# Linear attention and a squared-ReLU FFN on one core: a reordered start, empty matmuls in TensorE's waits, six output buffers and a last sum in three column runs

## The chip, the cores and the metric

The kernel runs on one core of a Trainium2 chip. A core has TensorE (matrix multiply, PE in the profile; its weight loads are PEld), VectorE (DVE), ScalarE (ACT), GpSimd (POOL) and SyncE (SP, which only issues DMAs here). TensorE writes to PSUM, which here is eight banks of 128 x 512 fp32; VectorE and ScalarE read it. The metric is the device time of the core in microseconds (us), given as the median of runs without a profile.

## The reference

Four batches of eight heads, 768 steps, head size 48. Each head keeps a 48 x 48 state:

```python
for t in range(S):
    cur = einsum('bhd,bhe->bhde', u * kt, vt)
    y[:, :, t] = einsum('bhd,bhde->bhe', rt, state + cur)
    state = w * state + einsum('bhd,bhe->bhde', kt, vt)
x = y.transpose(0, 2, 1, 3).reshape(3072, 384)
h = maximum(x @ w_in, 0)          # w_in 384 x 2048
out = h * h @ w_out               # w_out 2048 x 384
```

## The kernel before

The 768 steps are cut into six chunks of 128, so with four batches there are 24 *units*, numbered chunk by chunk: units 0 to 3 are the first chunk of each batch. A unit's 128 rows of x are 128 tokens of the FFN.

The whole program is one written list, `ORDER`. Each word is a step of one engine, `name.unit:engine/buffers`: `Y.0:P/5` is step Y of unit 0 on TensorE (P) into bank 5; D is VectorE, A ScalarE, G GpSimd, S SyncE. A loop at the end of the kernel calls the function of that name in class `Do`. So the list gives the order in each engine's queue, and each engine works its queue strictly in that order; semaphores hold a step until its inputs are there and its buffer is free. Nothing is rearranged by a scheduler.

The attention part of one unit:

- `ld.r`, `ld.k`, `ld.v` (L388) load 192 KB each. `rh`, `kh` (L434, L428) scale r and k by powers of w; `P0`, `P1`, `du` (L437, L441, L444) form sum(r * u * k) per head and `dv` (L449) multiplies it with v; `vb` (L286 on ScalarE, L288 on VectorE and GpSimd) is v in bf16.
- `T` (L464) transposes scaled r and k on TensorE into PSUM and `Tc` copies them out; later units use a transposing DMA, `XB`, instead.
- `A` (L494) makes the 128 x 128 products of each head, the heads of even number in one bank and those of odd number in another; `Bm` (L507, VectorE, one for each of the two banks) masks them. "Block A of unit 2" is `A.2`.
- `Y` (L531) multiplies the masked blocks with v, and from unit 4 on adds the state's part (L527); `xs` (L560, VectorE) adds dv and gives x; `U` (L552) makes the unit's update of the state.
- `X` (L578) transposes x on TensorE and `xTc` copies it out; later units use a DMA, `xX` (L585).

The FFN goes by groups: unit 0, unit 1, then two units at a time. `F1.g.s` (L594) makes four 128-wide blocks of the hidden layer (two where the group has two units), `re` (L602, L604) applies ReLU, `sq` (L609, L613) squares, `F2` (L622) sums over the hidden layer in PSUM, `os` copies the sum to a buffer in SBUF (pool `os`), and `out` (L667) stores it. The last unit to be summed, 22, is done by `F2c` (L636), column run by column run, so that the first run is copied and stored while the next is summed.

The weights arrive in the start: `lW.0.s` (L396) loads a 384 KB piece of w_in into one of six staging buffers and `cW.0.s` casts it to bf16 into W1_s. A staging buffer is loaded again only when its cast is done: `lW.0.3` uses the buffer of `lW.0.5` and so follows `cW.0.5`. W1_2 and w_out are loaded by GpSimd's DMAs (L418 to L422).

`Z.n.b` (L648, L650) is empty work: matmuls of the identity into bank b, n / 4 of them 512 columns wide and the remainder 128 wide. The kernel before has Z.66.7 and Z.22.7 ahead of T.3 and A.0.

Of the kernel before, what the change touches and what calls it, by code (L numbers as in the profile page):

```python
# [22 lines left out]
POOLS = dict(ldr=7, ldk=7, ldv=7, st=6, rk=7, P0=5, dv=5, vb=8, rkT=7, Bm=6, xs=5, hr=6, hq=30, os=4, ts=2, xT1=2, xT2=3)  # L23
# [57 lines left out]
P0.17:G/0 P1.17:G ts.16:D/0 du.17:D/2 sq.8.6:A0/28 F2.12.0.4:P/6 os.12:D/3 S.16:G Bm.17.0:D/1 U.13:P/3 ts.13:D/0 ld.v.19:S/5  # L81
# [3 lines left out]
re.8.4:A/3 F2.14.4.4:P/7 F2.15.12.4:P/1 F2.14.0.4:P/7 S.15:D ld.v.20:S/3 sq.8.4:A0/8 F2.15.8.4:P/1 os.15:A/2 U.14:P/2  # L85
ts.14:D/0 F2.14.8.4:P/7 os.14:A/0 kh.22:G/2 Bm.19.1:D/4 xX.17:S/1 F1.9.2:P/3 P1.21:G re.9.2:A/2 F1.9.6:P/5 re.9.6:A/4
# [7 lines left out]
F1.10.1:P/7 re.10.3:A/2 XB.22:S/6 os.16:D/2 Bm.20.1:D/4 sq.10.3:D2/11 re.10.1:A/5 F2.17.12.4:P/2 ld.v.22:S/0 os.17:D/1  # L94
# [4 lines left out]
S.18:G Y.22:P/7 F2.18.12.4:P/0 os.18:A/3 F1.11.4:P/2 re.11.4:A/5 P0.22:D/1 P1.22:D du.22:D/2 du.23:D/4 F1.11.6:P/5  # L99
# [3 lines left out]
F1.12.0:P/5 sq.11.0:D2/26 F2.20.0.4:P/1 F1.12.2:P/2 re.12.2:D/5 F1.11.3:P/7 re.11.2:A/1 sq.11.2:A0/3 os.19:D/0 F2.21.0.4:P/4  # L103
# [3 lines left out]
os.20:A/2 out.20:S F2.23.0.4:P/7 F2.23.8.4:P/7 os.23:D/0 os.21:A/3 out.21:S F2c.22.0:P/2 os.22.0:D/1 F2c.22.1:P/6 os.22.1:D/1  # L107
out.23:S out.22.0:A out.22.1:S
# [12 lines left out]
def kernel(  # L121
# [13 lines left out]
    B, H, S, D = r.shape  # L135
# [5 lines left out]
    d_model, d_ff = moe_w_in.shape  # L141
# [171 lines left out]
    class Do:  # L313
# [315 lines left out]
        def F2c(e, i, h):  # L629
            g, j = group_of[i]  # L630
            n = len(GROUP[g])
            m = 4 // n
            c = part(h)
            for f in range(FCH):
                at = L * n * (f % m) + L * j
                e.matmul(  # L636
                    bank(f"bO{i}{h}")[:, c],
                    hqb[slot[f"hq{g},{f // m}"]][:, at : at + L],
                    W2[f // 4][:, f % 4, c],
                    start=(f == 0), stop=(f == FCH - 1), skip_group_check=True,  # L640
                )
# [10 lines left out]
        def os(e, i, half=None):  # L652
            c = part(half)
            o = f"bO{i}" if half is None else f"bO{i}{half}"
            copy(e, osb[slot[f"os{i}"]][:, c], bank(o)[:, c])

        def out(e, i, half=None):
            c = part(half)
            t = osb[slot[f"os{i}"]]
            if i < PAIRED:  # L660
                o = bass.AP(
                    tensor=out.tensor, offset=out.offset + ((i - i % 2 + half) * S + i % 2) * d_model,
                    ap=[[2 * d_model, L // 2], [1, d_model]],
                )
                e.dma_start(out=o, in_=t[rows[half], :])
            else:
                e.dma_start(out=out_v[(i % B) * NCH + i // B][:, c], in_=t[:, c])  # L667
# [56 lines left out]
```

## Time and profile before

| | |
|---|---|
| median of three runs | 173.69 us (172.4 to 175.07) |
| profiled execution | 171.62 us |
| its span, first to last instruction | 169.9 us |
| mean granted TensorE clock | 0.99 |
| TensorE busy | 160.1 us, 94% |
| VectorE busy | 140.3 us, 83% |
| ScalarE busy | 104.4 us, 61% |
| GpSimd busy | 87.4 us, 51% |
| moved by DMA | 29.13 MB, mean 171 GB/s |

Start times in the profile are microseconds from the first instruction. A timeline row has start, duration, engine, line, operation, output <- input, and the number of instructions merged into it; behind it stands, in brackets, the idle time of the engine ahead of it and who ended that. "Granted clock" is TensorE's clock as a share of full speed. Durations of matmuls include the drain of the last one, so rows of TensorE overlap a little.

### The profile page before, as it was taken

The page shows a single profiled execution, that of the slowest core. Times are in us where ns is not written, and L with a number is a line of the kernel's source. Part 1 is how long each engine was busy: PE and PEld are TensorE (multiplying, and loading weights), DVE is VectorE, ACT ScalarE, POOL GpSimd, SP SyncE. Part 2 cuts the span into 40 slices and gives each one's busy share as a digit, 9 for nine tenths or more (in the row PEclk, how much of TensorE's full clock was granted, in tenths as well). Part 3 has the DMA queues.
Part 4 walks back from the last instruction along what each step waited for, and adds up shares of the span by engine and source line. Part 5 has one row for each costly group of instructions (what it writes and reads, how often), then busy time and mean ns, then how long its engine had stood idle before and what let it go on. Part 6 is the DMA issues. An engine that isn't in the chain of part 4 may idle for free.

```text
span 169.9 us, 4338 instructions
## 1 busy us (share of the span) xinstructions
PE 160.1 (94%) x1691; PEld 121.2 (71%) x1691; DVE 140.3 (83%) x272; ACT 104.4 (61%) x187; POOL 87.4 (51%) x105
## 2 busy tenths in 40 slices
PE   3974999999999999999999989999999999999993
PEld 1443888867787777787786776977786785878872
DVE  5599978869999997798999899899879889682731
ACT  3566497791799483766398273695595544644640
POOL 5427966308584699994649104869722862000000
PEclk9999699999999999999999999999999999999999
DMA  5999999997698999999979897999973954120422
GB/s 102 226 257 309 315 206 205 218 209 146 117 220 135 223 205 247 228 173 205 228 151 215 198 175 153 218 160 221 133 160 80 138 116 132 25 80 0 143 93 93
DMA packets 105588, 29.13 MB, mean 171 GB/s; under 512 B 98008, under 2 KB 105568, under 8 KB 105568
## 3 DMA queue, kind: packets, MB, share of 16 engines
q1 hardware_dynamic: 103272, 26.56, 77.0%
q0 software_dynamic: 1744, 1.77, 6.5%
q10 hardware_dynamic: 552, 0.53, 1.1%
q8 instruction: 13, 0.21, 0.5%
q14 instruction: 7, 0.06, 0.1%
HBM read 20.46 MB, written 4.72 MB: 148 GB/s over the span
## 4 chain that ended last, share of the span: by engine, by line
PE 78%; DMA 9%; DVE 4%; ACT 3%; issue 2%; POOL 1%; SPq 1%; POOLq 0%
PE bank L622 32%; PE bank L594 32%; PE bank L494 3%; DMA st<-in_moe_w_in_dram 3%; DMA ldv<-in_v_dram 2%; PE bank L531 2%; DMA ldk<-in_k_dram 2%; DMA rkT<-rk 2%; PE bank L578 2%; PE bank L527 2%; PE bank L552 2%; PE bank L636 2%; PE bank L464 1%; DVE Bm L507 1%; ACT rkT L286 1%
## 5 line engine op out<-in xcount | busy, mean ns | idle before, releaser
L594 PE MATMUL bank<-xT,W 128*128 128x256 bf16 (+1 forms) x624 | 71.1, 265 | 0.0
L622 PE MATMUL bank<-W,hq 128*128 128x384 bf16 x368 | 68.7, 326 | 0.1
L594 PEld LDWEIGHTS <-W 128*128 128x128 bf16 x624 | 56.2, 98 | 8.4 <-DVE W L288 0.2
L602 ACT ACTIVATE hr<-bank 128x512 bf16<-128x512 f32 x70 | 40.6, 593 | 25.8 <-PE bank L594 25.2
L609 ACT ACTIVATE hq<-hr 128x512 bf16<-128x512 bf16 x72 | 43.6, 627 | 7.8 <-DVE hr L604 6.6
L622 PEld LDWEIGHTS <-hq 128*128 128x128 bf16 x368 | 34.1, 98 | 18.6 <-ACT hq L609 0.7
L507 DVE TENSOR_TENSOR Bm<-bank,maskJT 128x512 bf16<-128x512 f32 x48 | 31.1, 679 | 0.9 <-PE bank L494 0.9
L604 DVE TENSOR_SCALAR hr<-bank 128x512 bf16<-128x512 f32 x26 | 17.6, 686 | 10.3 <-PE bank L594 9.5
L441 POOL TENSOR_TENSOR P<-P,ub 128x384 f32<-128x384 f32 x14 | 14.7, 1051 | 17.4 <-DVE P L437 17.0
L434 POOL TENSOR_TENSOR rk<-ldr,Wt 128x384 bf16<-128x384 f32 x13 | 14.2, 1094 | 5.3 <-DMA ldr<-in_r_dram 5.3
L449 POOL TENSOR_TENSOR dv<-ldv,du 128x384 f32<-128x384 f32 x16 | 13.6, 856 | 4.0 <-DVE du L444 3.7
L560 DVE TENSOR_TENSOR xs<-bank,dv 128x384 bf16<-128x384 f32 x24 | 13.1, 551 | 2.2 <-PE bank L531 0.7
L286 ACT COPY os<-bank 128x384 f32<-128x384 f32 x13 | 5.9, 483 | 13.5 <-PE bank L622 13.5
L573 POOL TENSOR_TENSOR S0W<-ts,WLm 128x384 bf16<-128x384 f32 x9 | 9.4, 1051 | 8.6 <-DVE ts L570 8.5
L428 POOL TENSOR_TENSOR rk<-ldk,Wkhat 128x384 bf16<-128x384 f32 x12 | 13.0, 1089 | 0.4 <-DMA ldk<-in_k_dram 0.3
L444 DVE TENSOR_REDUCE du<-P 128x8 f32<-128x384 f32 x24 | 12.9, 544 | 0.2
L613 DVE TENSOR_TENSOR hq<-hr 128x512 bf16<-128x512 bf16 x24 | 12.5, 525 | 0.4
L531 PE MATMUL bank<-vb,Bm 128*128 128x48 bf16 x192 | 11.5, 186 | 1.1 <-ACT vb L286 1.1
L288 POOL CAST vb<-ldv 128x384 bf16<-128x384 f32 x10 | 5.7, 568 | 13.1 <-DMA ldv<-in_v_dram 13.1
L437 POOL TENSOR_TENSOR P<-ldr,ldk 128x384 f32<-128x384 f32 x10 | 10.3, 1031 | 3.1 <-DMA ldr<-in_r_dram 3.1
L531 PEld LDWEIGHTS <-Bm 128*128 128x128 bf16 x192 | 9.8, 98 | 2.1 <-DVE Bm L507 1.2
L494 PE MATMUL bank<-rkT 48*128 48x128 bf16 x192 | 8.0, 221 | 2.4 <-ACT rkT L286 1.8
(67 smaller groups left out, 161.0 us busy)
## 6 DMA issues: line engine op xcount, KB each, us to landing
ldr<-in_r_dram SPq DMA_DIRECT2D x24, 192.0 KB, 3.7
ldk<-in_k_dram SPq DMA_DIRECT2D x24, 192.0 KB, 3.6
ldv<-in_v_dram SPq DMA_DIRECT2D x24, 192.0 KB, 4.2
out_dram<-os SPq DMA_DIRECT2D x23, 192.0 KB, 2.3
st<-in_moe_w_in_dram SPq DMA_DIRECT2D x6, 384.0 KB, 5.4
W<-in_moe_w_out_dram POOLq DMA_DIRECT2D x4, 384.0 KB, 6.5
st<-in_moe_w_in_dram ACTq DMA_DIRECT2D x1, 384.0 KB
rkT<-rk SPq DMA_TRANSPOSE x17, 3.7
```

The lines of the kernel that those rows point to most:

```text
L434: e.tensor_mul(scaled("r", i), loaded("r", i), early("WtQ") if i < EARLY else Wt2)
L441: e.tensor_mul(t, t, ub)
L449: e.tensor_mul(dvb[slot[f"dv{i}"]], loaded("v", i), t)
L494: e.matmul(heads(bank(f"bA{i}{h}"), 128)[:, hc, :], t[p0 : p0 + D, HP + hc, :], t[p0 : p0 + D, hc, :], start=True, stop=True, skip_group_c ...
L507: e.tensor_mul(o, a, mask_b)
L531: e.matmul(y[:, hc, D * h : D * (h + 1)], m[h][:, hc, :], vb[:, 2 * hc + h, :], start=(i < B), stop=True, skip_group_check=True,)
L560: e.tensor_add(xsb[slot[f"xs{i}"]].rearrange("p (a b) -> p a b", a=HP), heads(bank(f"bY{i}"), 2 * D), dvb[slot[f"dv{i}"]].rearrange("p (a ...
L594: e.matmul(hp[:, fi, :], W1[f // 2][:, c, 128 * (f % 2) : 128 * (f % 2 + 1)], xt[:, c, :], start=(c == 0), stop=(c == CCH - 1), skip_group ...
L602: e.activation(hr, hp, AF.Relu)
L604: e.tensor_scalar_max(hr, hp, 0.0)
L609: e.activation(hq, hr, AF.Square)
L622: e.matmul(bank(f"bO{i}")[:, 0:d_model], hqb[slot[f"hq{g},{f // m}"]][:, at : at + L], W2[f // 4][:, f % 4, :], start=(summed[i] == 1), st ...
```

## The change

Four things change.

1. The order of the first units. On VectorE, `Bm.0.0` comes ahead of `Bm.1.0`, and `xs.0` (the sum of unit 0) ahead of both Bm of unit 3. On TensorE, `A.2` comes ahead of `U.0`, and `X.0` (the transpose that gives x of unit 0) ahead of `Y.3`; X.0 and Y.1 use other banks. On ScalarE, `vb.0` and `Tc.2` come ahead of `cW.0.5`.
2. Five new empty steps: Z.20.7 ahead of A.1, Z.10.6 ahead of A.3, Z.8.0 ahead of U.3, Z.8.5 ahead of Y.0, Z.8.2 ahead of Y.3; in all 13 matmuls of 512 columns and 2 of 128.
3. The pool `os` has six buffers for four, and the steps take them in turn.
4. F2c of unit 22 is done in three column runs of 192, 128 and 64 for two of 256 and 128. The second run is copied and stored by ScalarE, the first and third by VectorE and SyncE.

```diff
-POOLS = dict(ldr=7, ldk=7, ldv=7, st=6, rk=7, P0=5, dv=5, vb=8, rkT=7, Bm=6, xs=5, hr=6, hq=30, os=4, ts=2, xT1=2, xT2=3)
+POOLS = dict(ldr=7, ldk=7, ldv=7, st=6, rk=7, P0=5, dv=5, vb=8, rkT=7, Bm=6, xs=5, hr=6, hq=30, os=6, ts=2, xT1=2, xT2=3)
...
-A.0:P/4/5 ld.k.2:S/3 WtS:A lW.0.5:A/1 P1.3:G kh.1:D/2 lW.0.1:S/0 rh.1:D/2 T.1:P/6 Tc.1:A/1 A.1:P/7/3 Tc.3:A/2 A.3:P/6/2 ld.v.0:S/0
+A.0:P/4/5 ld.k.2:S/3 WtS:A lW.0.5:A/1 P1.3:G kh.1:D/2 lW.0.1:S/0 rh.1:D/2 T.1:P/6 Tc.1:A/1 Z.20.7:P A.1:P/7/3 Tc.3:A/2 Z.10.6:P A.3:P/6/2 ld.v.0:S/0
...
-        return slice(0, d_model) if half is None else (slice(0, 256), slice(256, d_model))[half]
+        return slice(0, d_model) if half is None else (slice(0, 192), slice(192, 320), slice(320, d_model))[half]
```

The first place is VectorE's queue where the Bm steps of units 0, 1 and 3 stand. Bm_0 and Bm_2 are the two blocks of unit 0 (Bm.0.1 and Bm.0.0), Bm_1 and Bm_5 those of unit 1, Bm_3 and Bm_4 those of unit 3; xs_0 and xs_1 are the sums of units 0 and 3, and xT1_0 is x of unit 0, transposed. Before:

```order
L507 TENSOR_TENSOR Bm_0_121<-bank_5_190,maskJT_239 128x512
L507 TENSOR_TENSOR Bm_1_122<-bank_7_192,maskJT_239 128x512
L507 TENSOR_TENSOR Bm_2_123<-bank_4_189,maskJT_239 128x512
L507 TENSOR_TENSOR Bm_3_124<-bank_2_187,maskJT_239 128x512
L507 TENSOR_TENSOR Bm_4_125<-bank_6_191,maskJT_239 128x512
L560 TENSOR_TENSOR xs_0_127<-bank_5_190,dv_0_101 128x384
L507 TENSOR_TENSOR Bm_5_126<-bank_3_188,maskJT_239 128x512
L560 TENSOR_TENSOR xs_1_128<-bank_2_187,dv_1_102 128x384
L288 COPY xT1_0_132<-bank_6_191 128x384
```

After (the last number of a name only counts buffers, and is two higher behind the new ones):

```order
L507 TENSOR_TENSOR Bm_0_121<-bank_5_192,maskJT_241 128x512
L507 TENSOR_TENSOR Bm_2_123<-bank_4_191,maskJT_241 128x512
L507 TENSOR_TENSOR Bm_1_122<-bank_7_194,maskJT_241 128x512
L560 TENSOR_TENSOR xs_0_127<-bank_5_192,dv_0_101 128x384
L507 TENSOR_TENSOR Bm_3_124<-bank_2_189,maskJT_241 128x512
L507 TENSOR_TENSOR Bm_4_125<-bank_6_193,maskJT_241 128x512
L507 TENSOR_TENSOR Bm_5_126<-bank_3_190,maskJT_241 128x512
L560 TENSOR_TENSOR xs_1_128<-bank_2_189,dv_1_102 128x384
L288 COPY xT1_0_132<-bank_5_192 128x384
```

The sum of unit 0 moved from the sixth place to the fourth; the copy of its transposed x stays ninth.

The second place is ScalarE's queue at the same time: rkT_1, rkT_2 and rkT_3 are the copies Tc of units 1, 3 and 2, vb_1 is vb.0, W1_5 and W1_0 are cW.0.5 and cW.0.0. Before:

```order
L286 COPY rkT_1_115<-bank_6_191 128x1024
L286 COPY rkT_2_116<-bank_2_187 128x1024
L286 CAST W1_5_198<-st_1_180 128x768
L286 CAST vb_1_107<-ldv_0_77 128x384
L286 COPY rkT_3_117<-bank_1_186 128x1024
L286 CAST W1_0_193<-st_2_181 128x768
```

After:

```order
L286 COPY rkT_1_115<-bank_6_193 128x1024
L286 COPY rkT_2_116<-bank_2_189 128x1024
L286 CAST vb_1_107<-ldv_0_77 128x384
L286 COPY rkT_3_117<-bank_1_188 128x1024
L286 CAST W1_5_200<-st_1_182 128x768
L286 CAST W1_0_195<-st_2_183 128x768
```

The cast of the weight piece W1_5 moved behind the two copies that had stood behind it.

The third place is the end of SyncE's queue, the last stores (os_1 is the buffer of unit 22 in both). Before:

```order
L667 DMA out_0_dram<-os_1_174 128x384
L667 DMA out_0_dram<-os_2_175 128x384
L667 DMA out_0_dram<-os_3_176 128x384
L667 DMA out_0_dram<-os_0_173 128x384
L667 DMA out_0_dram<-os_1_174 128x128
```

After:

```order
L667 DMA out_0_dram<-os_5_178 128x384
L667 DMA out_0_dram<-os_2_175 128x384
L667 DMA out_0_dram<-os_3_176 128x384
L667 DMA out_0_dram<-os_1_174 128x192
L667 DMA out_0_dram<-os_1_174 128x64
```

The first run of unit 22 is now stored by SyncE, which ended with a run of 128 columns and now ends with one of 64; the run that ScalarE stores is 128 columns wide and was 256.

More of the change, by code (lines that the diff above doesn't have):

```diff
@@ L106 @@
 re.12.1:D/5 F1.12.5:P/5 sq.12.1:D2/0 F2.20.4.4:P/1 re.12.6:A/4 sq.12.6:A0/4 F2.23.12.4:P/7 re.12.5:A/2 sq.12.5:A0/12 out.17:S
-os.20:A/2 out.20:S F2.23.0.4:P/7 F2.23.8.4:P/7 os.23:D/0 os.21:A/3 out.21:S F2c.22.0:P/2 os.22.0:D/1 F2c.22.1:P/6 os.22.1:D/1
-out.23:S out.22.0:A out.22.1:S
+os.20:A/5 out.20:S F2.23.0.4:P/7 F2.23.8.4:P/7 os.23:D/3 os.21:A/2 out.21:S F2c.22.0:P/2 os.22.0:D/1 F2c.22.1:P/6 os.22.1:A/1 F2c.22.2:P/0 os.22.2:D/1
+out.23:S out.22.0:S out.22.1:A out.22.2:S
 """
```

30 lines of the change are left out of this document (15 added, 15 removed).

## The prediction

> **What bounds the kernel now.** I read the page's busy line and its slices first, then the list of who waited for whom on TensorE, then a table of time windows over the start, and last the timelines of the engines there. Four rows of the page:
>
> ```profile
> PE 160.1 (94%) x1691; PEld 121.2 (71%) x1691; DVE 140.3 (83%) x272; ACT 104.4 (61%) x187; POOL 87.4 (51%) x105
> ...
> PE   3974999999999999999999989999999999999993
> ...
> DVE  5599978869999997798999899899879889682731
> ...
> PEclk9999699999999999999999999999999999999999
> ```
>
> The second row is TensorE in 40 slices of 4.25 us: after the fifth slice it is full until the last one. All its waits on other engines are these (total us, times, longest):
>
> ```profile
> PE bank L494 <- ACT rkT L286: 1.8, 3, 1.1
> PE bank L531 <- ACT vb L286: 1.1, 1, 1.1
> PE bank L494 <- DMA rkT<-rk: 0.5, 1, 0.5
> PE bank L552 <- POOL vb L288: 0.5, 1, 0.5
> ```
>
> Only the 0.5 us for a DMA lies behind the start. So the kernel is a TensorE stream with a start in front and a tail behind: a microsecond won before the stream is full moves the end, and so does one won in the tail; nothing between has room. The windows over the start (columns: PE, PEld, DVE, ACT, POOL busy with instruction counts, granted clock, DMA share, GB/s):
>
> ```profile
> 9.50:12.90 3.40, 2.28 (x31) 1.29 (x28) 3.37 (x9) 2.85 (x4) 1.00 (x1) 1.00 1.13 270
> 12.90:16.35 3.45, 1.33 (x27) 1.17 (x28) 3.45 (x7) 1.94 (x4) 2.63 (x5) 1.00 1.14 309
> 16.35:19.75 3.40, 3.19 (x48) 2.60 (x45) 3.40 (x8) 1.88 (x3) 3.32 (x4) 0.51 1.14 314
> 19.75:23.20 3.45, 3.43 (x66) 3.25 (x63) 3.45 (x7) 2.70 (x7) 2.54 (x4) 0.99 1.21 257
> ```
>
> Two readings. TensorE is busy only 1.33 of 3.45 us in the second window, and in the third it is granted half its clock. And VectorE is busy through all of the last three. The second reading decides what the first is worth. VectorE's timeline (start, us, line, out<-in):
>
> ```profile
> 13.31 0.94 DVE L288 CAST W<-st 128x768 bf16<-128x768 f32 x1
> 14.17 3.07 DVE L507 TENSOR_TENSOR Bm<-bank,maskJT 128x512 bf16<-128x512 f32 x5
> 17.16 0.55 DVE L560 TENSOR_TENSOR xs<-bank,dv 128x384 bf16<-128x384 f32 x1
> 17.63 0.68 DVE L507 TENSOR_TENSOR Bm<-bank,maskJT 128x512 bf16<-128x512 f32 x1
> 18.23 0.54 DVE L560 TENSOR_TENSOR xs<-bank,dv 128x384 bf16<-128x384 f32 x1
> 18.69 0.34 DVE L288 COPY xT<-bank 128x384 bf16<-128x384 bf16 x1
> ...
> 21.36 1.80 DVE L288 CAST W<-st 128x768 bf16<-128x768 f32 x2
> 23.08 0.55 DVE L560 TENSOR_TENSOR xs<-bank,dv 128x384 bf16<-128x384 f32 x1
> 24.06 0.36 DVE L288 COPY xT<-bank 128x384 bf16<-128x384 bf16 x1 [0.44 <-PE bank L578]
> ```
>
> Each row starts before the one ahead has ended; the first idle time is the 0.44 us at 24.06. And TensorE:
>
> ```profile
> 9.15 1.24 PE L648 MATMUL bank<-identity 128*128 128x512 bf16 x5
> 14.44 0.61 PE L464 MATMUL bank<-identity,rk 128*128 128x128 bf16 x8
> 16.20 0.38 PE L531 MATMUL bank<-vb,Bm 128*128 128x48 bf16 x8 [1.15 <-ACT vb L286]
> 19.12 1.17 PE L594 MATMUL bank<-xT,W 128*128 128x128 bf16 x12
> 23.69 0.34 PE L578 MATMUL bank<-identity,xs 128*128 128x128 bf16 x3
> 23.86 4.78 PE L594 MATMUL bank<-xT,W 128*128 128x128 bf16 x54
> ```
>
> The first F1 (19.12) starts when VectorE's copy of xT (18.69 + 0.34) is done, and the transposes X.2 (23.69) when VectorE's xs.2 (23.08 + 0.55 = 23.63) is done. From 23.86 TensorE has its work lined up. **The start ends at 23.86, and VectorE, not TensorE and not its clock, sets that moment.**
>
> **Part 1, the order of unit 0.** On VectorE the change permutes the stretch from 14.17 to 19.03: six Bm, two xs and one xT copy, the same nine before and after, and everything behind stays. A queue that never waits ends at the same time in any order, so the gain at 23.86 is 0, unless a moved step now waits. The two that could: xs.0 is now fourth. The five Bm take (3.07 - 0.68) / 4 = 0.60 us each, so the second (Bm.0.0) ends at 14.17 + 0.60 + 0.68 = 15.45 and the third at 16.05. Y.0 needs Bm.0.0 and vb.0; it takes 0.38 us from about 15.5, so its sum is there at 15.9, before the third Bm ends. xs.3 stays where it was (18.23), but its Y.3 starts only when Bm.3.0 ends, now sixth: 17.16 + 0.55 = 17.71. With 0.38 us for Y.3 that is 18.1 at full clock: 0.1 us to spare. Price 0; bounds 0 to +0.4 (both waits, at half clock).
>
> **Part 2, the empty matmuls.** Five wide ones took 1.24 us with the last one's drain, about 0.21 each, narrow ones a quarter of that. Added are 1.07 us ahead of A.1 (wait 1.1), 0.54 ahead of A.3 and 0.43 ahead of U.3 (waits of about 0.5 each), and 0.43 ahead of Y.0, behind T.2 (about 14.9) and Bm.0.1 (14.85), so done by 15.3 to 15.4, before 15.5. The last 0.43 stand ahead of Y.3, behind the read of Bm.3.1 (about 17.1): done by 17.6, before 17.71. Behind each in TensorE's queue stands the very step that waits anyway. Price 0. What they buy is busy time in the window 12.90 to 16.35: 1.33 + 0.43 + 0.43 for those of U.3 and Y.0, part of A.3's, and Y.0 and A.2 moved into it, some 2.7 of 3.45, above the 2.28 after which the clock stayed. So I expect a clock of 1.0 from 16.35 to 19.75. F1.0.0 then takes about 0.7 instead of 1.17 us, and TensorE waits that much longer for VectorE at 23.2: again 0. On when the clock falls, the Trainium skill (TensorE: Matmul & The Clock Gate, section Why this matters for your kernels) asks for no idle gap above about 3 us. Here the longest is 1.15 us and the clock fell all the same, so busy share, not the gap, is what I go by; by the rule the empty matmuls would change nothing, and the sum would be the same.
>
> **Part 3, ScalarE and the queue of SyncE.** vb.0 moves from behind cW.0.5 to ahead of it, and cW.0.5 behind Tc.2:
>
> ```profile
> 11.42 1.93 ACT L286 COPY rkT<-bank 128x1024 bf16<-128x1024 bf16 x2 [0.55 <-PE bank L464]
> 14.85 0.88 ACT L286 CAST W<-st 128x768 bf16<-128x768 f32 x1 [1.51 <-DMA st<-in_moe_w_in_dram]
> 15.64 0.51 ACT L286 CAST vb<-ldv 128x384 bf16<-128x384 f32 x1
> 16.05 1.01 ACT L286 COPY rkT<-bank 128x1024 bf16<-128x1024 bf16 x1
> ```
>
> vb.0 can run from 13.35; Tc.2 when T.2 is done (14.44 + 0.61 = 15.05), to about 16.1; cW.0.5 then ends at 16.95 instead of 15.73. cW.0.0 behind it starts at 16.95 in both. But cW.0.5 frees the staging buffer into which SyncE loads lW.0.3, and all of SyncE's later loads queue behind that one:
>
> ```profile
> 16.18 1.30 SPq L396 DMA_DIRECT2D st<-in_moe_w_in_dram  x1
> ```
>
> It could not start before about 16.95: 0.75 us of hold. Its data is first needed by cW.0.3 on GpSimd, and that by F1.2.3:
>
> ```profile
> 23.36 0.82 POOL L288 CAST W<-st 128x768 bf16<-128x768 f32 x1 [1.05 <-DMA st<-in_moe_w_in_dram]
> ```
>
> In the run of 54 F1 matmuls from 23.86, F1.2.3 comes behind 12 narrow and 6 wide ones, a share of 1.3 us by columns (24 narrow and 30 wide fill 4.6), so at 25.2. cW.0.3 ended at 24.18 and would end at 24.93: 0.25 us to spare. Price 0, bounds 0 to +1.05 (the 1.30 of that issue added to the hold, less the 1.0 of slack).
>
> **Part 4, six output buffers.** The list of waits names no copy to os that waited for a store: the ones on record wait for TensorE. Only addresses and slots change; I take 0, and a gain or loss is bounded by the absence of such a wait, so 0 both ways.
>
> **Part 5, the tail.** F2c.22 runs in 256 and 128 columns now, and in 192, 128 and 64 after:
>
> ```profile
> 164.39 2.65 PE bank L636 x32
> ```
>
> That is the chain's row; the copies, the last issue and the landings (kind, count, size, us from the issue) are:
>
> ```profile
> 166.18 0.42 DVE L288 COPY os<-bank 128x256 f32<-128x256 f32 x1 [1.19 <-PE bank L636]
> 167.07 0.29 DVE L288 COPY os<-bank 128x128 f32<-128x128 f32 x1 [0.47 <-PE bank L636]
> ...
> 167.39 0.33 SPq L667 DMA_DIRECT2D out_dram<-os  x1
> ...
> out_dram<-os ACTq DMA_DIRECT2D x1, 128.0 KB, 1.7
> out_dram<-os SPq DMA_DIRECT2D x1, 64.0 KB, 1.5
> ```
>
> The columns are the same 384 per row of weights, 16 times; 2.65 us over 16 x 384 columns is 0.43 ns a column. 16 more matmuls cost at least nothing and, at the 8 matmuls of 48 columns in 0.38 us shown at 16.20 (48 ns each, drain included), at most 16 x (48 - 28) = 0.3 us; I take 0.05, near the first, since loads overlap. The last copy shrinks from 128 to 64 columns: 0.13 us between 256 and 128, so about 0.065 less: 0.22. SyncE's issue and landing then follow as before (0.33, and 1.5 or a little less for half the bytes). The middle piece goes out on ScalarE's queue: matmuls done at 164.39 + 1.33 + 0.88 = 166.6, copy about 0.3, issue about 0.4, landing 1.7: 169.0, before the last piece's 169.2. Price 0.05 - 0.065 = -0.01; bounds -0.2 to +0.3.
>
> **The sum.** 0 + 0 + 0 + 0 - 0.01: the profiled execution stays at a span of 169.9 and 171.62 us. It was the fastest of the four on record (172.40, 173.69, 175.07 beside it; their mean is 173.2, the median given is 173.69), so with no effect I would expect a new median near 173.2; I take 0.2 off for executions in which the clock falls at a worse place (rival C). **Forecast: 173.0 us.**
>
> **Rivals.**
> A. *TensorE paces the start after all.* If VectorE's rows could close up (as they cannot by the row of 3.45 busy of 3.45), the half clock's 3.19 us of work would cost 1.6 less: 171.4. For it speaks the 0.51 clock; against it the 24.06 row. Chance 0.17.
> B. *The hold on SyncE bites: slower.* lW.0.3 lands later than cW.0.3's slack allows, TensorE stops ahead of F1.2.3, and the loads of units 4 and 5 are late behind it. It decides from a hold of 1.0 us; price up to 1.05: 174.0. For it: cW.0.3 already waits 1.05 us for that load. Against: DMA shares above 1 mean a backlog, in which a late issue loses less than it is late. Chance 0.13.
> C. *The place of the clock's fall differs from one execution to the next, and the empty matmuls remove the bad ones.* The second spell of full clock began at this weight load, and 16.35 lies three spells of 3.42 us behind it:
>
> ```profile
> 6.09 1.43 PEld L648 LDWEIGHTS <-identity 128*128 128x128 bf16 x7 [0.28 <-issue]
> ```
>
> Were the half clock two microseconds later, to 21.75, TensorE would lose another 1.0, less some 0.2 of waiting at 23.2: 0.8. Without it 172.2. The Trainium skill (TensorE: Matmul & The Clock Gate, Part 1: The HAM clock gate) has a window of 3413 ns that runs freely and does not start with the kernel; the spacing here agrees, its shift between executions no run here shows. Chance 0.10.
> D. *The change doesn't do what it says*: the clock falls all the same, the empty matmuls take twice as long, Y.3 and xs.3 come 0.4 late: 173.4. Chance 0.05.
>
> The forecast has 0.55. The range is 171.0 to 175.0: it takes in A to D, the bounds of parts 1, 3 and 5, and the runs' own spread of 2.7 us, of which a median of three keeps the larger part. Two per cent is 3.5 us, about what a measurement of this kernel can tell from no change; no case reaches it, so within 2% has 0.92, and the runs' spread leaves 0.04 on each side (below 170.2, above 177.2).
>
> **What the profile after would show.** Right: granted clock 1.0 in the fifth slice; TensorE's L648 rows ending before A.1, A.3, U.3, Y.0, Y.3 start; VectorE without idle time from 8.5 to 23.6, xs.2 ending near 23.6 and the long F1 run starting near 23.9; SyncE's load of lW.0.3 starting near 17.0; the last output copy 0.22 us. Wrong: an xs.2 that ends before 23.2 (A), a wait of PEld for GpSimd's W near 25 (B), an idle VectorE ahead of xs.0 or xs.3 (D), or a later part of the stream that moves although nothing in it was touched.

## The result, and the profile after

The changed kernel takes 174.03 us in the median of 20 runs (172.82 to 176.61), the kernel before 173.19 us in 20 runs beside it (171.76 to 176.73). The ratio is 1.0055, with a 95% interval of 1.0032 to 1.0078: slower by half a per cent, some 0.9 us. I had forecast no change (173.0 us). The profiled execution took 173.70 us, with a span of 172.0 us. Executions more than 1.5% above the fastest of their kernel are left out of every ratio below, and profiles taken in one are left out of the table and the readings.

The page of the changed kernel, busy time and slices as before:

```profile
PE 162.8 (95%) x1722; PEld 121.5 (71%) x1722; DVE 139.4 (81%) x272; ACT 104.6 (61%) x188; POOL 88.4 (51%) x105
...
PE   3996899999999999999999799999999999999993
...
PEclk9999999999999999999999999999999999999999
```

The empty matmuls hold the clock, as forecast: TensorE is fuller in the third and fourth slices, and its granted clock never falls. The windows over the start (columns as before):

```profile
12.90:16.35 3.45, 2.58 (x30) 1.51 (x31) 3.45 (x7) 1.13 (x3) 1.65 (x3) 1.00 1.02 292
16.35:19.75 3.40, 2.56 (x43) 1.52 (x42) 3.08 (x7) 2.33 (x3) 3.32 (x5) 1.00 1.09 308
```

Granted clock 1.00 where it had been 0.51, and 2.58 us of work where there had been 1.33. But VectorE, busy 3.40 of 3.40 us in the second of these windows before, is now busy 3.08. Its timeline says why:

```profile
14.61 1.88 DVE L507 TENSOR_TENSOR Bm<-bank,maskJT 128x512 bf16<-128x512 f32 x3
16.81 0.56 DVE L560 TENSOR_TENSOR xs<-bank,dv 128x384 bf16<-128x384 f32 x1 [0.33 <-POOL dv L449]
17.29 1.88 DVE L507 TENSOR_TENSOR Bm<-bank,maskJT 128x512 bf16<-128x512 f32 x3
...
23.91 0.55 DVE L560 TENSOR_TENSOR xs<-bank,dv 128x384 bf16<-128x384 f32 x1
```

The row at 16.81 is xs.0 in its new place. It waits 0.33 us, and the input that came last was dv.0 on GpSimd, done at 16.78. xs.2 then starts at 23.91 (23.08 before), and the long F1 run at 24.70 (23.86 before):

```profile
24.52 0.34 PE L578 MATMUL bank<-identity,xs 128*128 128x128 bf16 x3
24.70 4.78 PE L594 MATMUL bank<-xT,W 128*128 128x128 bf16 x54
```

The long run is 0.84 us later. Of that, 0.44 was there already when the first Bm started (14.61 for 14.17; nothing ahead of it on VectorE was changed, and the executions differ there), the other 0.40 comes between. The chain that ended last, over this stretch, names the same steps (start, us, what):

```profile
8.77 5.88 DMA ldv<-in_v_dram
14.65 0.05 issue
14.70 0.50 POOL vb L288
15.21 1.58 POOL dv L449 x2
16.79 0.02 issue
16.81 0.56 DVE xs L560
17.37 1.79 DVE Bm L507 x3
19.17 0.46 DVE xs L560
```

The load of v of unit 3, vb.3, dv.3 and dv.0 on GpSimd, then xs.0: in its new slot the sum of unit 0 hangs on the landing of the data of unit 3, because GpSimd works vb.3 and dv.3 ahead of dv.0. TensorE's Y.0, the other input of xs.0, was hardly earlier:

```profile
15.43 0.61 PE L464 MATMUL bank<-identity,rk 128*128 128x128 bf16 x8
15.87 0.59 PE L648 MATMUL bank<-identity 128*128 128x512 bf16 x2
16.31 0.36 PE L531 MATMUL bank<-vb,Bm 128*128 128x48 bf16 x8
```

The last row is Y.0, done at 16.67. Its Bm.0.0 had been done at 15.89 (14.61 + 0.60 + 0.68). But U.3, ahead of T.2 (15.43), had waited 0.9 us for vb.3, and then the two empty matmuls Z.8.5 stood ahead of Y.0: they cost it some 0.4 us, from 15.89 to 16.31. In kernels below where xs.0 does wait for Y.0, it starts 0.10 to 0.11 us behind Y.0's end; here that would be 16.77 or 16.78. So dv.0 and Y.0 were late by nearly the same amount, and both stand behind vb.3.

In the kernel before the chain of the same stretch does not touch VectorE's xs.0:

```profile
16.14 0.92 ACT rkT L286
17.07 0.05 issue
17.11 0.61 PE bank L494 x6
17.72 0.43 PE bank L531 x8
18.15 0.32 PE bank L578 x3
18.47 0.35 PE bank L531 x8
```

Behind 24.70 the changed kernel loses more. Of TensorE's waits (total us, times, longest)

```profile
PE bank L594 <- DMA xT<-xs: 1.6, 3, 1.0
PE bank L552 <- POOL vb L288: 0.9, 1, 0.9
```

the second is that of U.3 in the start, but all three parts of the first lie behind 24.70, the longest at 97.66 us; it is new. From the start of the long F1 run to that of F2c the profile before has 140.37 us and this one 141.77, 1.40 more. In the tail little moves: F2c started at 164.23 before and 166.47 after (+2.24), the last copy ended at 167.36 and 169.58 (+2.22), and from the start of F2c to the end of the span it is 5.67 us before and 5.53 after.

```profile
166.47 2.84 PE L636 MATMUL bank<-W,hq 128*128 128x192 bf16 x48
...
169.35 0.23 DVE L288 COPY os<-bank 128x64 f32<-128x64 f32 x1 [1.00 <-PE bank L636]
```

### The profile page after: what moved, and what is told of

Read it like the earlier page. It is cut to its first block, busy times and chain, and to the rows that moved or that the text cites. A ratio compares the mean times of both kernels' runs of the same rounds, so it can differ in the third digit from the quotient of the medians.

```text
span 172.0 us, 4403 instructions
## 1 busy us (share of the span) xinstructions
PE 162.8 (95%) x1722; PEld 121.5 (71%) x1722; DVE 139.4 (81%) x272; ACT 104.6 (61%) x188; POOL 88.4 (51%) x105
## 4 chain that ended last, share of the span: by engine, by line
PE 56%; DVE 11%; issue 11%; DMA 9%; POOL 6%; SPq 3%; ACT 1%; DVEq 0%; POOLq 0%
PE bank L594 25%; PE bank L622 22%; DVE Bm L507 4%; DMA xT<-xs 4%; DMA ldv<-in_v_dram 3%; SPq L388 3%; DMA ldr<-in_r_dram 2%; PE bank L494 2%; DVE xs L560 2%; PE bank L636 2%; PE bank L531 1%; POOL P L437 1%; POOL rk L434 1%; PE bank L527 1%; DVE W L288 1%
## 5 line engine op out<-in xcount | busy, mean ns | idle before, releaser
L286 ACT COPY os<-bank 128x384 f32<-128x384 f32 (+1 forms) x14 | 6.2, 468 | 16.6 <-PE bank L622 13.8
L437 POOL TENSOR_TENSOR P<-ldr,ldk 128x384 f32<-128x384 f32 x10 | 10.9, 1097 | 3.8 <-DMA ldr<-in_r_dram 3.8
L648 PE MATMUL bank<-identity 128*128 128x512 bf16 x34 | 10.1, 434 | 2.8 <-POOL identity masks.py:199 2.7
L613 DVE TENSOR_TENSOR hq<-hr 128x512 bf16<-128x512 bf16 x24 | 12.0, 506 | 0.3
L531 PE MATMUL bank<-vb,Bm 128*128 128x48 bf16 x192 | 11.0, 183 | 0.2 <-DVE Bm L507 0.2
```

Source lines behind the costliest of these rows:

```text
L531: e.matmul(y[:, hc, D * h : D * (h + 1)], m[h][:, hc, :], vb[:, 2 * hc + h, :], start=(i < B), stop=True, skip_group_check=True,)
```

## The experiments

Each kernel was timed in 12 runs, beside 23 to 35 runs of the kernel before on the same chip; the interval of a ratio is some 0.4% to either side, nearly as much as the effect, so I lean on groups of kernels and on what each profile shows at one place.

### First group: which of the four edits

Theory O: the new order of the first units costs. Theory Z: the empty matmuls cost. Theory S: the six buffers or the column runs cost. Theory H: within O, the later cast cW.0.5 holds SyncE's load lW.0.3 and what queues behind it. (Where these expectations speak of P, it is the chain over GpSimd from vb.3 to the weight loads it issues.)

**e1_order**, the new order alone:

```diff
-ld.v.3:S/1 ... cW.0.5:A T.2:P/1 cW.0.1:D
-Bm.0.1:D/0 Bm.1.0:D/1 vb.0:A/1 Tc.2:A/3 Bm.0.0:D/2 Y.0:P/5 U.0:P/7 Bm.3.1:D/3 A.2:P/1/4 Bm.3.0:D/4 ld.v.1:S/2 Y.3:P/2 dv.0:G
-xs.0:D/0 lW.0.0:S/2 X.0:P/6 ...
+ld.v.3:S/1 ... vb.0:A/1 T.2:P/1 cW.0.1:D Tc.2:A/3 cW.0.5:A
+Bm.0.1:D/0 Bm.0.0:D/2 Y.0:P/5 Bm.1.0:D/1 A.2:P/1/4 U.0:P/7 dv.0:G xs.0:D/0 X.0:P/5 Bm.3.1:D/3 Bm.3.0:D/4 ld.v.1:S/2
+Y.3:P/2 lW.0.0:S/2 ...
```

> The new order of the start alone: no empty matmuls, four output buffers, the last sum in two runs as before. Theory W (xs.0, moved ahead, waits on VectorE for GpSimd's dv.0; 0.33 us in the trace after): slower by 0.2 to 0.6%, and an idle VectorE ahead of xs.0. Theory H (cW.0.5 behind Tc.2 holds SyncE's load of lW.0.3, the loads behind it leave 1 to 2 us later, and transposing DMAs of the middle are late): slower by 0.4 to 0.8%, with SyncE's wc at about 18.4 instead of 17.6 and over 1 us of TensorE waits for DMA. Theory Z (the empty matmuls cost) and theory S (buffers and tail cost): within 0.2% of before.

Measured: 174.55 us for 173.64; ratio 0.9992 (0.9951 to 1.0032). Not resolved by itself: the median of all twelve executions is 0.9 us up, the ratio, to which six of them count, is not.

**e2_empty**, the five empty steps alone:

```diff
+Z.20.7:P   ahead of A.1
+Z.10.6:P   ahead of A.3
+Z.8.0:P    ahead of U.3
+Z.8.5:P    ahead of Y.0
+Z.8.2:P    ahead of Y.3
```

> Only the five empty steps, at the same five places of the old order. Theory Z: slower by 0.4% or more, with steps of the start that begin later behind L648. Theories W, H, S: within 0.2% of before, with a granted clock of 1.0 from 16.35 to 19.75 and the long F1 run at 23.9 all the same, since VectorE sets it; if TensorE's half clock did cost something, faster by up to 0.5%.

Measured: 173.6 for 173.64 us; ratio 0.9983 (0.9949 to 1.0017). No cost or gain that can be measured: Z is not borne out.

**e3_os_tail**, the six buffers and the three column runs alone:

```diff
-... os=4 ...
+... os=6 ...
-F2c.22.1:P/6 os.22.1:D/1 out.23:S out.22.0:A out.22.1:S
+F2c.22.1:P/6 os.22.1:A/1 F2c.22.2:P/0 os.22.2:D/1 out.23:S out.22.0:S out.22.1:A out.22.2:S
```

> Only the six output buffers and the three column runs of the last sum; the start as before. Theory S: slower by 0.4% or more, from stores or from the tail. Theories W, H, Z: within 0.2% of before, the tail (start of F2c to the end of the span) within 0.2 us of before's 5.5 us.

Measured: 172.92 for 173.64 us; ratio 0.9976 (0.9942 to 1.001). S falls. No other kernel came out lower, but the kernel before, measured once more as c1 below, is at 0.9978.

**e4_cast_first**, the whole change with cW.0.5 ahead of Tc.2:

```diff
-vb.0:A/1 T.2:P/1 cW.0.1:D Tc.2:A/3 cW.0.5:A
+vb.0:A/1 T.2:P/1 cW.0.1:D cW.0.5:A Tc.2:A/3
```

> The whole change, but with ScalarE's cast cW.0.5 ahead of Tc.2 (vb.0 stays ahead of both), so that SyncE's load of lW.0.3 is not held. Theory H: the loss goes (within 0.2% of before), wc at about 17.6. Theory W: the loss stays, 0.3 to 0.8% slower than before, with VectorE idle ahead of xs.0. Theories Z and S: the loss stays too.

Measured: ratio 1.0057 (1.0022 to 1.0091). The loss stays, so H is not borne out.

### Second group: the edits in pairs

**e7_empty_os_tail** is the change without the new order, **e8_order_os_tail** without the empty matmuls, **e9_order_empty** without buffers and column runs, **e10_again** the changed kernel unaltered. The edits are those above, combined.

> The change without its new order: the empty matmuls, the six buffers and the three column runs over the old order of the start. Theory O (the new order of the start is what costs, whatever in it): 0.1 to 0.5% faster than before. Theory X (only order and empty matmuls together cost, each alone is harmless): within 0.3% of before. Theory Z (the empty matmuls cost): 0.3% or more slower.

> The change without its empty matmuls: new order, six buffers, three column runs. Theory O: slower than before by 0.2 to 0.6%. Theory X: within 0.3% of before. Theory Z: within 0.3% of before or faster. The granted clock falls to a half for one or two spells of 3.4 us as in before.

> The new order and the empty matmuls, with four buffers and two column runs. Theories O and X: as slow as the whole change or a little slower, 0.4 to 0.8%. Theory S (buffers or tail cost): within 0.3% of before.

> The whole change once more, beside the three others on the same chip, and with a second trace of it: 0.3 to 0.8% slower than before by every theory. In its trace theory W wants VectorE idle ahead of xs.0 for GpSimd's dv.0 again; theory P (GpSimd's whole queue is late behind the load of v for unit 3, and with it the load of the first piece of w_out) wants the first F2 row to start at the moment that load lands, not when the 54 F1 matmuls end.

Measured: e7 1.0022 (0.9987 to 1.0057), e8 1.0063 (1.002 to 1.0107), e9 1.0038 (0.9991 to 1.0084), e10 1.0043 (0.9999 to 1.0086). The three with the new order are up, two of them with an interval that reaches 1; the one without it is not resolved from no change. X falls by e8. O fits best, but it is not shown here: it had e7 faster than the kernel before, and the interval of e7 overlaps those of the other three.

### Third group: which part of the order

Theory V: xs.0, now early on VectorE, waits for dv.0. Theory A: ScalarE's order. Theory P from here on: what is left, Bm.0.0 ahead of Bm.1.0 and A.2 ahead of U.0.

**e5_dv0**, the whole change with dv.0 first on GpSimd:

```diff
-ld.v.3:S/1 vb.3:G/0 ...
+ld.v.3:S/1 dv.0:G vb.3:G/0 ...
-... U.0:P/7 dv.0:G xs.0:D/0
+... U.0:P/7 xs.0:D/0
```

> The whole change, with dv.0 put ahead of vb.3 on GpSimd, so that it is done before the data of v of unit 3 has to be there. Theory V (the new order costs because xs.0, now early on VectorE, waits for dv.0 on GpSimd): no idle time of VectorE ahead of xs.0, the long F1 run starts some 0.3 us earlier against the first Bm (9.7 for 10.1 us), and the time is 0.0 to +0.4 us from the kernel before. Theory A (the order of ScalarE costs) and theory P (the order of TensorE and of the Bm): no idle time ahead of xs.0 either, but the time stays at +0.7 us.

Measured: ratio 1.0053 (1.0013 to 1.0093). And xs.0 still waits, longer than in the changed kernel, and for another engine:

```profile
17.23 0.56 DVE L560 TENSOR_TENSOR xs<-bank,dv 128x384 bf16<-128x384 f32 x1 [0.81 <-PE bank L531]
```

TensorE explains it. U.3 stands ahead of T.2 and Y.0 in its queue and needs vb.3, which GpSimd now does behind dv.0:

```profile
15.71 0.33 PE L552 MATMUL bank<-vb,rk 128*128 128x96 bf16 x4 [0.94 <-POOL vb L288]
...
16.76 0.36 PE L531 MATMUL bank<-vb,Bm 128*128 128x48 bf16 x8
```

Behind U.3 come T.2 and Z.8.5, two empty matmuls that stand ahead of Y.0 from 16.33 to 16.76 here, though Bm.0.0 was done at 15.83. So dv.0 was only one of two inputs of xs.0 that are just in time; with it out of the way, Y.0 is the late one, by its place behind vb.3 and, for 0.43 us of the 0.81, by the empty step. My claim that e5 would have no idle time ahead of xs.0 was wrong.

**e11_xs_late**, the whole change with xs.0 and X.0 back in their old places:

```diff
-... dv.0:G xs.0:D/0 X.0:P/5 Bm.3.1:D/3 Z.8.2:P Bm.3.0:D/4 ld.v.1:S/2
-Y.3:P/2 ...
+... dv.0:G Bm.3.1:D/3 Z.8.2:P Bm.3.0:D/4 xs.0:D/0 ld.v.1:S/2
+Y.3:P/2 X.0:P/5 ...
```

> The whole change, with xs.0 back behind both Bm of unit 3 on VectorE, and X.0 behind Y.3 on TensorE; the order of ScalarE and the rest stay new. Theory V: xs.0 stands where dv.0 has long been done, so the time is 0.0 to +0.3 us from the kernel before. Theories A and P: +0.7 us.

Measured: 175.4 for 174.54 us; ratio 1.0031 (0.9994 to 1.0069). xs.0 has no wait, but the time does not decide: the interval holds both no change and the whole loss.

**e12_act_old**, the whole change with cW.0.5 ahead of vb.0 and Tc.2 as before:

```diff
-du.1:D/2 vb.0:A/1 T.2:P/1 cW.0.1:D Tc.2:A/3 cW.0.5:A
+du.1:D/2 cW.0.5:A vb.0:A/1 T.2:P/1 cW.0.1:D Tc.2:A/3
```

> The whole change, with ScalarE's order as before (cW.0.5 ahead of vb.0 and Tc.2). Theory A: 0.0 to +0.2 us from the kernel before. Theories V and P: +0.7 us. vb.0 is then done at about 16.1, so Y.0 and xs.0 come later than in the kernel changed, and by V the stall ahead of xs.0 is as long or longer, only with TensorE as the one waited for.

Measured: ratio 1.0076 (1.0042 to 1.011); xs.0 waits 0.58 us for Y.0, as V has it. A alone falls.

**e13_dv0_later**, the whole change with dv.0 behind vb.1 on GpSimd:

```diff
-U.0:P/7 dv.0:G xs.0:D/0 ... vb.1:G/2 Bm.1.1:D/5
+U.0:P/7 ld.v.1:S/2 vb.1:G/2 dv.0:G xs.0:D/0 ... Bm.1.1:D/5
```

> The whole change, with the suspected wait made longer: dv.0 stands behind vb.1 on GpSimd (0.5 us, or more where v of unit 1 lands late). Theory V: VectorE waits 0.8 to 1.2 us ahead of xs.0, the long F1 run starts 10.5 to 10.9 us behind the first Bm, and the time is +1.2 us from the kernel before. Theories A and P: the wait is there, but the time stays at +0.7 us.

Measured: 177.48 us for 174.54; ratio 1.009 (1.0037 to 1.0142), some 1.6 us, from five of the twelve executions. The sign is V's, but the interval reaches down into that of the changed kernel, so that this wait goes to the end in full is not shown.

### Fourth group: a control, P, and the later waits

Theory M: the loss is made in the middle, by the wait near 97 us for the transposed x of unit 12.

**c1_before** is the kernel before, measured as if it were changed. **e14_bm_a2** is the kernel before with P alone:

```diff
-Bm.0.1:D/0 Bm.1.0:D/1 vb.0:A/1 Tc.2:A/3 Bm.0.0:D/2 Y.0:P/5 U.0:P/7 Bm.3.1:D/3 A.2:P/1/4 Bm.3.0:D/4
+Bm.0.1:D/0 Bm.0.0:D/2 vb.0:A/1 Tc.2:A/3 Bm.1.0:D/1 Y.0:P/5 A.2:P/1/4 U.0:P/7 Bm.3.1:D/3 Bm.3.0:D/4
```

> The kernel before, unchanged, measured like a changed one. If the measurement is fair: 0 +- 0.5 us. If the kernel that stands beside the kernel before is slower by itself: +0.7 us. For theory M its profile counts too: by M the wait of the long stream for the transposed x of unit 12, near 97 us, is absent or under 0.3 us, as in the first profile of this kernel; if it is there with about 1 us, that wait is the execution's and not the change's.

> The kernel before with one part of the new order alone: Bm.0.0 ahead of Bm.1.0 on VectorE and A.2 ahead of U.0 on TensorE. Theory P: +0.7 us. Theory M and theories of several small parts: 0 to +0.3 us.

Measured: c1 0.9978 (0.9934 to 1.0022), no difference from itself; e14 0.9992 (0.9962 to 1.0023), so P falls. c1's profile tells something of the baseline that the first profile had not. Its windows:

```profile
12.90:16.35 3.45, 2.01 (x28) 1.49 (x28) 3.45 (x7) 1.76 (x3) 2.08 (x3) 0.80 1.00 276
16.35:19.75 3.40, 2.54 (x40) 2.11 (x41) 3.40 (x7) 2.48 (x4) 2.48 (x4) 0.50 1.12 317
19.75:23.20 3.45, 3.45 (x46) 3.45 (x47) 3.13 (x7) 1.73 (x4) 3.43 (x5) 0.71 1.05 269
```

The same program had a lowered clock in three of these windows here, and in one in its first profile. In the last of them VectorE is busy only 3.13 us and TensorE all of 3.45: in this execution TensorE does hold the start.

**e15_xx_early** and **e16_os_tail_xx**: the transposing DMA of unit 12 ahead of two loads on SyncE, in the whole change and in e3:

```diff
-ld.v.15:S/3 ld.r.16:S/5 vb.15:A/0 ld.k.19:S/3 ... xX.12:S/2 F1.7.7:P/0
+ld.v.15:S/3 vb.15:A/0 ... xX.12:S/2 ld.r.16:S/5 ld.k.19:S/3 F1.7.7:P/0
```

> The whole change, with the transposing DMA of unit 12 issued ahead of two loads on SyncE (r of unit 16, k of unit 19) instead of behind them. Theory M: it lands some 2 us earlier, the wait of 1.0 us near 97 us is gone, and the time is -0.3 to 0.0 us from the kernel before. Theory P or a loss in the start: the wait is gone but another takes part of its place, and the time stays at +0.4 to +0.7 us.

> The old order of the start without empty matmuls, six output buffers, three column runs, and the transposing DMA of unit 12 ahead of the two loads. By M, where the old order does not have the wait, this gains nothing over the same kernel with the loads in front (-0.5 us from the kernel before); if the wait is in most executions of every kernel, it gains another 0.5 to 1.0 us.

Measured: e15 1.0064 (1.0025 to 1.0102), e16 1.0019 (0.9981 to 1.0057). e16 is no lower than e3. In e15 the wait near 97 us is gone; TensorE then waits 1.49 us at 103.16 for the next transposing DMA:

```profile
103.16 0.62 PE L494 MATMUL bank<-rkT 48*128 48x128 bf16 x16 [1.49 <-DMA rkT<-rk]
```

In this execution the wait only moved. M, as a cause at that place, is not borne out.

### Fifth group: the two parts left, each alone

**e17_act_alone**, ScalarE's new order on the kernel before (the diff of e12 the other way round), and **e18_xs_alone**, the early xs.0 and X.0 on the kernel before:

```diff
-... U.0:P/7 Bm.3.1:D/3 A.2:P/1/4 Bm.3.0:D/4 ld.v.1:S/2 Y.3:P/2 dv.0:G
-xs.0:D/0 lW.0.0:S/2 X.0:P/6 ...
+... U.0:P/7 dv.0:G xs.0:D/0 X.0:P/5 Bm.3.1:D/3 A.2:P/1/4 Bm.3.0:D/4 ld.v.1:S/2 Y.3:P/2
+lW.0.0:S/2 ...
```

> The kernel before with ScalarE's new order alone: vb.0 and Tc.2 ahead of cW.0.5. Theory A (the later cast holds SyncE's load lW.0.3 and the loads behind it): lW.0.3 issued after 17 us, +0.5 to +0.8 us. Theory V (the early xs.0): 0 to +0.2 us. If each piece is enough for the loss: +0.5 to +0.8 us here and in the other run.

> The kernel before with the early xs.0 on VectorE and X.0 on TensorE alone. vb.0 is then done only near 16.1 us, so xs.0 waits some 0.5 us for TensorE's Y.0. Theory V: that wait goes to the end, +0.4 to +0.8 us. Theory A: 0 to +0.2 us. If neither run is above +0.3 us, the loss comes only from the pieces together, and stays without a place.

Measured: e17 1.0005 (0.9966 to 1.0043); e18 1.0083 (1.005 to 1.0116), 176.08 for 174.82 us. **The early xs.0, with its X.0, is enough for a loss of that size over the old order.** Whether it is the same loss is another matter. In e18 xs.0 stands right behind the Bm that Y.0 waits for, vb.0 stands behind cW.0.5, and X.0 stands ahead of A.2, none of which holds in the changed kernel. e18's chain over the start:

```profile
11.27 4.37 DMA st<-in_moe_w_in_dram
15.64 0.02 issue
15.66 0.02 ACT W L286
15.68 0.77 issue
16.46 0.52 ACT vb L286
16.97 0.04 issue
17.01 0.49 PE bank L531 x8
...
17.60 0.56 DVE xs L560
18.16 1.79 DVE Bm L507 x3
```

Here the landing of a weight piece (lW.0.5, whose cast stands ahead of vb.0 on ScalarE), vb.0, Y.0 and xs.0 set the pace. In the old place the same lateness meets a VectorE that still has two Bm to do. But from 20.56 on e18's chain runs over TensorE alone, and TensorE has half its clock there:

```profile
16.35:19.75 3.40, 2.18 (x32) 1.54 (x32) 2.73 (x5) 2.41 (x4) 3.32 (x5) 0.52 1.07 312
19.75:23.20 3.45, 3.30 (x37) 3.04 (x35) 3.04 (x8) 1.08 (x2) 3.41 (x5) 0.50 0.97 253
```

Nor is that only this execution's: the mean granted clock of the whole program is 0.97 in 9 of the 11 executions of e18 that count, and 0.98 in 18 of the 19 of the kernel before beside it. Where TensorE sets the pace, 0.009 of 174 us is some 1.6 us (an estimate from these clocks), which is as much as the whole loss of e18. The changed kernel has a clock of 0.99 to 1.00 in every execution. So part of e18's loss, perhaps all, can be a clock that the changed kernel does not have; no run separates the two.

### All profiles side by side

"Start" is the time from the first Bm on VectorE to the long F1 run, "later" the sum of TensorE's waits over 0.1 us behind 30 us:

| kernel | xs.0 early | empties | ratio | first Bm | start | later |
|---|---|---|---|---|---|---|
| before | no | no | 1 | 14.17 | 9.69 | 0.55 |
| c1 | no | no | 0.9978 | 14.97 | 10.23 | 2.02 |
| e3 | no | no | 0.9976 | 14.42 | 10.13 | 1.65 |
| e14 | no | no | 0.9992 | 15.85 | 9.90 | 1.57 |
| e7 | no | yes | 1.0022 | 15.74 | 9.67 | 1.99 |
| e11 | no | yes | 1.0031 | 14.66 | 9.93 | 1.79 |
| after | yes | yes | 1.0055 | 14.61 | 10.09 | 1.59 |
| e4 | yes | yes | 1.0057 | 14.95 | 9.72 | 2.11 |
| e5 | yes | yes | 1.0053 | 14.55 | 10.84 | 2.50 |
| e9 | yes | yes | 1.0038 | 15.05 | 9.69 | 2.54 |
| e12 | yes | yes | 1.0076 | 15.03 | 10.34 | 2.64 |
| e15 | yes | yes | 1.0064 | 14.90 | 9.71 | 2.73 |
| e1 | yes | no | 0.9992 | 15.14 | 11.03 | 0.96 |
| e8 | yes | no | 1.0063 | 14.96 | 10.85 | 3.05 |
| e18 | yes | no | 1.0083 | 15.05 | 11.12 | 1.45 |

With e10 (early) and e2, e16 and e17 (late), whose times alone count, the ten kernels with an early xs.0 have ratios of 0.9992 to 1.0083, mean 1.0052; the eight with a late one 0.9976 to 1.0031, mean 1.0001. In the column "start" the smallest value is 9.67 to 9.72 in both kinds: when nothing waits, the order is neutral. e13, whose wait was made longer, is left out of these means. So as groups they differ by half a per cent.

The wait at xs.0 does not explain that. Without empty matmuls the mean of "start" is 11.0 for 10.0 us, with them 10.1 for 9.8; but VectorE waits for an input of xs.0 by more than 0.2 us in only four of the nine profiles with an early xs.0, and three of these are e5, e12 and e18, which differ from the changed kernel in what makes an input late (dv.0 first, or vb.0 behind the cast). In e1 and e8 it is TensorE at half clock that lengthens the start (0.50 from 19.75 to 23.20 in both). The early xs.0 as the changed kernel has it, with the empty matmuls, vb.0 ahead of the cast and dv.0 in its place, is in four profiles: after, e4, e9 and e15. Only the first has the wait. This is e9:

```profile
15.05 1.88 DVE L507 TENSOR_TENSOR Bm<-bank,maskJT 128x512 bf16<-128x512 f32 x3
16.86 0.56 DVE L560 TENSOR_TENSOR xs<-bank,dv 128x384 bf16<-128x384 f32 x1
```

xs.0 starts before the Bm ahead of it has ended, and the start is 9.69 to 9.72 us in e4, e9 and e15, within 0.05 us of the smallest. Yet their ratios are 1.0038 to 1.0064, and the profiled executions of e4 and e9 were not lucky ones (174.66 and 175.25 us, where the medians of their kernels are 173.99 and 175.28). Whatever these executions lose, they do not lose it between the first Bm and the long F1 run. From the long F1 run to F2c they take 142.8 to 143.2 us. That stretch is 140.4 and 142.3 in the two profiles of the kernel before, 141.4 to 142.6 in the other four with a late xs.0, and 140.8 to 143.5 in the other six with an early one.

How narrow the new slot is can be read off. xs.0 can start 1.8 us behind the first Bm in its new place (16.77 - 14.96 in e8, where nothing held it). dv.0 ends at 16.78 in the changed kernel, 2.2 us behind its first Bm, and in the first profile of the kernel before at 15.79, 1.6 us behind:

```profile
14.18 1.61 POOL L449 TENSOR_TENSOR dv<-ldv,du 128x384 f32<-128x384 f32 x2
```

In the profiles of e3, e7 and e9 it is 1.5, 0.9 and 1.7 us. Of the 14 profiles in which GpSimd's order is the old one, two are beyond 1.8: the changed kernel and e11 (1.9). So dv.0 is late for the new slot now and then, not as a rule. The old slot is 3.0 us behind the first Bm (17.16 - 14.17), out of reach of that spread.

## Why the prediction was wrong

- **What bounds the kernel: half right.** "VectorE, not TensorE and not its clock, sets that moment" holds as a floor: e7, with the clock held at 1.0 and the old order, has 9.67 us for 9.69. But I built it on one execution, the fastest of the first four, in which half clock lasted one window. In c1, e3 and e14 the stage is 0.2 to 0.5 us longer than the floor, and the chain of the first profile itself went over ScalarE and TensorE; I had not read that view for the start.
- **Part 1 is the step that failed in the profiled execution.** The sentence "a queue that never waits ends at the same time in any order, so the gain at 23.86 is 0, unless a moved step now waits" stands; the price of 0 behind it does not. I left out one input of xs.0, dv.0 on GpSimd: 15.79 at its end against a slot at about 16.0, 0.2 us to spare, in a program whose first Bm alone starts at 14.17 to 15.85 us in the profiles. And I gave Y.0 a start at 15.5 from one set of arrival times, in which vb.3 does not hold U.3, T.2 and Z.8.5 ahead of it. In the profile after, dv.0 was done at 16.78 and Y.0 at 16.67, xs.0 waited 0.33 us, and the start was 0.40 us longer, at the top of my bounds of 0 to +0.4. That is one execution. In e4, e9 and e15 Y.0 and dv.0 came in time, as I had worked it out, and the start cost nothing.
- **The other step that failed is "nothing between has room".** I took the stream behind the start as full because one list of waits had only 0.5 us there. Behind 30 us TensorE waits 0.55 us in that profile, 2.02 in c1, the same program, and 1.59 after; from the long F1 run to F2c it is 140.37, 142.29 and 141.77 us. So a later part of the stream did move although nothing in it was touched, which the prediction itself had called a sign of being wrong. How much of the 0.9 us is lost in the start and how much behind it, no run settles. (The list also leaves out a wait of 2.7 us for the identity, at the very beginning; nothing hangs on it.)
- **Part 2: right on the clock and on the price, not on every place.** The clock is 1.00 from 16.35 to 19.75, the window has 2.58 us of work (2.7 expected), and nothing is gained: e2 0.9983, e7 1.0022. But "behind each stands the very step that waits anyway" failed for Z.8.5 in the profile after and in e5, where it held Y.0 by some 0.4 us.
- **Part 3: no cost found, though it went further than I wrote.** The hold on lW.0.3 was longer than I worked out. The two casts cW.0.5 and cW.0.0 on ScalarE, and lW.0.3 on SyncE:

```profile
16.98 1.69 ACT L286 CAST W<-st 128x768 bf16<-128x768 f32 x2
...
17.91 0.44 SPq L396 DMA_DIRECT2D st<-in_moe_w_in_dram  x1
```

lW.0.3 was issued at 17.91, not at 17.0, since Tc.2, which now stands ahead of cW.0.5, itself waited for T.2, and that for U.3 and vb.3. Yet TensorE did not wait for a weight cast by GpSimd. Alone (e17) and undone (e4, e12) it changes the ratio by nothing that can be measured.
- **Parts 4 and 5: right, within their bounds.** e3 0.9976 (0.9942 to 1.001); in the tail F2c took 2.84 us for 2.80, the last copy 0.23 us (0.22 expected), and the time to the end of that copy moved by -0.02 (-0.01 expected). The whole tail gained more: from the start of F2c to the end of the span it is 5.65 to 5.71 us in the six profiles with two column runs and 5.45 to 5.54 in the nine with three.
- **The rivals.** A (TensorE paces the start) and C (the clock's fall differs between executions) are right about the kernel before in executions like c1, but their gain did not appear in the times; e7 has the clock of 1.0 and 1.0022. B named the right sign, but e4 and e17 do not bear out its queue, SyncE's. D's clause "Y.3 and xs.3 come 0.4 late" looked at the right engine and, for the profile after, the wrong step.
- **The sum.** 173.0 was 1.0 us low. That the profiled execution was a lucky one I had seen (median about 173.2), and that was right: 173.19. The 0.2 us that I took off for a better clock did not come, and the other 0.84 us are the change's cost.

What stays open is the cause of the 0.9 us. Shown are a wait at xs.0 in one execution, and a difference of half a per cent between ten kernels with an early xs.0 and eight with a late one. All ten but e18 also have the rest of the new order of VectorE and TensorE, which alone (e14) costs nothing that can be measured; e18, the one kernel with the early xs.0 alone, loses clock as well; and taking xs.0 back out of the changed kernel (e11) is not resolved either way. The waits behind 30 us are larger with the early xs.0 (means 2.2 and 1.6 us), but they range from 0.55 to 3.05 us between executions, and c1 alone differs from the first profile of the same program by 1.5 us. Whether they are a consequence of the start or chance isn't settled. No version measured is faster than the kernel before beyond its interval.

## What to carry to other kernels

Moving a step ahead on an engine that never idles is free only if every input of that step, from every engine, is there at the new slot. Write each input's end beside the slot, and measure the gap against how much arrivals shift from one execution to the next, not against zero: here the gap was 0.2 us, the arrivals shift by about a microsecond, and the old slot's gap of 1.4 us had covered all of it in the profiles. Before weighing an idle engine or a slow clock, read the chain over that stretch in more than one profile: one fast execution hides which engines are level, and how much the rest of the stream moves by itself. And when a part of a change is tried alone, see whether it loses its time in the same place as the whole: e18's loss had the right size and, by its clock, may be another one.

## What the runs showed of the hardware

- The granted clock of the unchanged kernel falls at different places in different executions: 0.51 in one window of 3.4 us in the first profile, and 0.80, 0.50 and 0.71 in three neighbouring ones in c1. The Trainium skill (TensorE: Matmul & The Clock Gate, Part 1: The HAM clock gate) describes a window of 3413 ns that runs freely and does not start with the kernel; a fall that lies shifted by part of a window from one execution to the next agrees with it.
- A transposing DMA that stands on SyncE's queue behind loads can take nearly twice as long to land in one execution as the same DMA behind the same loads in another, here of the other kernel. xX.12 was issued at 92.25 us in the first profile of the kernel before and at 92.15 in the changed kernel, behind the same six loads of 192 KB in both. The windows of the 2 us ahead of it, and the time to its landing, before:

```profile
90.25:92.25 2.00, 2.00 (x21) 1.25 (x18) 2.00 (x5) 1.48 (x4) 2.00 (x3) 1.00 1.07 209
...
DMA to landing us min/median/max: 2.9/2.9/2.9
```

And after:

```profile
90.15:92.15 2.00, 2.00 (x24) 1.34 (x22) 2.00 (x5) 2.00 (x5) 2.00 (x3) 1.00 1.39 218
...
DMA to landing us min/median/max: 5.5/5.5/5.5
```

The rate is nearly the same (209 and 218 GB/s), the DMA share is not (1.07 and 1.39): the packets ahead of it took longer. What made them take longer, no run here shows.
- A store of 64 columns (32 KB) at the end landed 1.5 us after its issue, no later than the 128 columns (64 KB) of the kernel before.
